# First loads, warm-up and K order at the start of a fused attention and MLP kernel

## The chip, the cores and the metric

The kernel runs on one NeuronCore of a Trainium2 chip. The metric is device time in microseconds (us) for one execution. Three runs of the kernel before gave 262.43, 262.99 and 263.99 us, so its median is 262.99 us.

## What is computed

The input `x` has 2048 rows of 640 numbers in bfloat16. Two branches read it and a gate mixes them:

```
g = sigmoid((x * gate_w).sum(-1))            # one number per row
a = linear_attention(x @ wqkv) @ wo          # 32 heads of 20, phi(q), phi(k)
b = x1 + gelu(layernorm(x1) @ w3) @ w4       # x1 = x + shifted gelu(layernorm(x) @ w1) @ w2
out = g * a + (1 - g) * b
```

with `phi(t) = where(t > 0, t + 1, exp(t)) + 1e-6`. Only the first stage of the attention branch matters here: K = x @ wk, and the gate's sum, which the kernel gets as one more column of the same product.

## The kernel before

**Stages.** The order of all work is written out by hand, with no planner: each engine executes its instructions in the order of the program text, and semaphores join the engines. TensorE (PE) goes through K (line 187), Q (line 233), the attention sums (line 310), then w1, w2, w3, the attention output and w4 in an interleaved order. The rows of `x` are handled in 16 chunks of 128.

**Loads.** Three queues can start transfers: SP (`sp`), ACT (`aq`) and GpSimd, called POOL in the profile (`gq`). A transfer is issued by its engine in program order. At the start the kernel wants natural-layout copies of chunks 0 and 1 of `x` (`load_x`, line 120), the 640-number gate vector as five rows of 128 (`g5`, line 129), and the K weights in five pieces of 128 rows (`load_wk`, line 126). Chunks 2 to 15 come transposed by DMA (`load_xT`, line 123), and behind them SP issues every later weight.

**Turning chunks 0 and 1.** K needs `x` transposed. A DMA transpose of the first chunks would land late, so PE turns chunks 0 and 1 by a product with an identity matrix (`turn`, line 206): five 128-column matmuls a chunk. The results go from PSUM to `xT` in two copies, the first two blocks of a chunk by one engine and the last three by another.

**The gate column.** `g5` is five rows; VectorE (DVE) copies it into a zeroed 128 by 128 tile `g5z` (lines 201 and 202). One small matmul (line 213) turns that into a column of five values in each partition, and ScalarE (ACT) copies it into column 640 of `wk_sb` (line 214). After that `k_mm` (line 183) makes K in two halves of 320 columns, the second with 321, the last of which is the gate's sum for each row. The identity comes from GpSimd (lines 153 and 154).

**Warm-up.** Before any of this PE runs matmuls on constant ones, whose results nobody reads (`warmup`, line 197): five of 512 columns and one of 384.

**Order on PE.** Warm-up; two blocks of chunk 0; the gate matmul; three blocks of chunk 0; five blocks of chunk 1; then K of chunks 0 and 1 by weight piece, pieces 0 to 4 in order, both chunks for each piece; then K of chunks 2 to 15. A PE instruction that waits holds everything behind it.

**Evacuation.** After each chunk `k_evac` (line 190) copies the gate sum out and applies `phi` with one ACT and two DVE instructions.

Of the kernel before, what the change touches and what calls it, by code (L numbers as in the profile page):

```python
# [16 lines left out]
def kernel(  # L17
# [13 lines left out]
    nc = tc.nc  # L31
    P = 128
# [7 lines left out]
    DC = D // P  # L40
# [30 lines left out]
    def pair():  # L71
        return ps.tile([P, 2, 512], F32, name="pp")
# [16 lines left out]
    g5 = const.tile([DC, P], BF16)  # L89
    g5z = const.tile([P, P], BF16)  # L90
# [26 lines left out]
    sp, aq, gq = nc.sync, nc.scalar, nc.gpsimd  # L117

    def load_x(c0, c1, q=sp):
        q.dma_start(x_sb[:, c0:c1, 0:D], x2[c0 * P:c1 * P, :].rearrange("(c p) d -> p c d", p=P))  # L120
# [4 lines left out]
    def load_wk(q, dc):  # L125
        q.dma_start(wk_sb[:, dc, 0:D], A_wqkv[dc * P:(dc + 1) * P, D:2 * D])

    load_x(0, 1)
    aq.dma_start(g5[:], gate_w.rearrange("(c p) -> c p", p=P))
    load_x(1, 2)  # L130
    load_wk(aq, 0)
    load_wk(sp, 1)
    load_wk(aq, 2)
    load_wk(sp, 3)
    load_wk(aq, 4)
    for c0, c1 in ((2, 3), (3, 4), (4, 5), (5, 6), (6, 8), (8, 10), (10, 12), (12, 16)):
        load_xT(c0, c1)
    sp.dma_start(wq_sb, wqkv_v[:, :, 0:D])
# [6 lines left out]
    for g in range(4):  # L145
        if g >= 2:
# [6 lines left out]
    nc.gpsimd.memset(ident[:], 1.0)  # L153
    nc.gpsimd.affine_select(out=ident[:], in_=ident[:], compare_op=ALU.is_equal, fill=0.0,
                            base=0, pattern=[[-1, P]], channel_multiplier=1)
    for c in range(0, NCH, CPT):
        nc.gpsimd.memset(x_sb[:, c:c + CPT, D:D + 1], 1.0)
    nc.gpsimd.memset(hmask[:], 1.0)
# [24 lines left out]
    def k_mm(pt, c, dcs):  # L183
        for dc in dcs:
            for hf in range(2):
                n = HD + hf
                nc.tensor.matmul(pt[:, hf, 0:n], lhsT=xT[:, dc, c * P:(c + 1) * P],  # L187
                                 rhs=wk_sb[:, dc, hf * HD:hf * HD + n], start=(dc == 0), stop=(dc == DC - 1))
# [5 lines left out]
    warm, tp, kps = pair(), pair(), [pair(), pair()]  # L194
    one = nc.const_aps.tensor(1.0, (P, TS), BF16)

    def warmup(n, w=TS):
        for i in range(n):
            nc.tensor.matmul(warm[:, 1, 0:w], lhsT=one[:, 0:P], rhs=one[:, 0:w], start=True, stop=True)

    nc.vector.memset(g5z[:], 0.0)
    nc.vector.tensor_copy(g5z[0:DC, :], g5[:])
    warmup(5)
    warmup(1, 3 * P)

    def turn(pt, c, a, b, copy):
        for dc in range(a, b):
            nc.tensor.matmul(pt[:, 0, (dc - a) * P:(dc - a + 1) * P], lhsT=x_sb[:, c, dc * P:(dc + 1) * P],  # L208
                             rhs=ident[:], start=True, stop=True)
        copy(xT[:, a:b, c * P:(c + 1) * P], pt[:, 0, 0:(b - a) * P].rearrange("p (c s) -> p c s", c=b - a))  # L210
# [2 lines left out]
    nc.tensor.matmul(kps[0][:, 0, 0:DC], lhsT=g5z[:], rhs=ident[:, 0:DC], start=True, stop=True)  # L213
    nc.scalar.copy(wk_sb[:, :, D], kps[0][:, 0, 0:DC])
    turn(kps[1], 0, 2, DC, nc.scalar.copy)
    turn(tp, 1, 0, 2, nc.vector.tensor_copy)
    turn(warm, 1, 2, DC, nc.vector.tensor_copy)
    for dc in range(DC):
        for c in range(2):
            k_mm(kps[c], c, (dc,))  # L220
    for c in range(2):
# [416 lines left out]
```

## Time and profile before

| what | value |
|---|---|
| median of the runs | 262.99 us (262.43 to 263.99) |
| profiled execution, device time | 264.31 us |
| its span, first to last instruction | 262.6 us |
| PE busy | 257.0 us, 98% of the span |
| DVE, ACT, POOL busy | 141.4, 83.3, 26.8 us |
| first matmul | 0.83 us from the span's start |
| first matmul of K | 5.47 us |
| first matmul of Q | 28.75 us |

Times inside the execution are counted from the span's first instruction. Besides the engines' busy times the profile gives a chain: it starts at the last instruction and goes back, step by step, to what released each. "Waits" list how long an engine sat idle and what ended it. A row of a group gives the number of instructions, their summed time and the mean time of one; matmuls overlap, so the distance between starts tells the rate and the listed duration is longer than that distance.

### The profile page before, as it was taken

Reading aid. Unit: us, or ns where it says so; the run is one execution under the profiler, and the core shown is the slowest. Engines: PE = TensorE matmul, PEld = TensorE weight load, DVE = VectorE, ACT = ScalarE, POOL = GpSimd, SP = SyncE. Lnnn points to the kernel's source line nnn. Section 1 sums busy time; section 2 is a strip of 40 time slices with the busy share of each in tenths; the row PEclk is TensorE's granted clock in tenths of the full one; section 3 lists DMA queues with packets and bytes.
Section 4 is the critical chain, followed back from the end, with each engine's and each line's share of the span. In section 5 each row is a group of like instructions: output and inputs, shape, how many; then the busy total and the mean of one; then the engine's idle time right before and its main releaser. Section 6 shows DMA issues by size and latency. Waiting matters only on the chain.

```text
span 262.6 us, 4149 instructions
## 1 busy us (share of the span) xinstructions
PE 257.0 (98%) x1649; PEld 159.4 (61%) x1667; DVE 141.4 (54%) x275; ACT 83.3 (32%) x126; POOL 26.8 (10%) x82
## 2 busy tenths in 40 slices
PE   7999999999999999999999999999999999999995
PEld 3677655688854644555577566567745567555543
DVE  2398778799947895776303478970312223112132
ACT  2455444412164535622420221140233350142100
POOL 3000040012220041031000023310000000000000
PEclk9999999999999999999999999999999999999999
DMA  7999988015656735998002011321200001100011
GB/s 197 182 182 378 365 246 317 0 27 100 125 115 84 189 91 118 180 317 90 6 2 75 25 27 25 75 54 25 76 26 0 0 2 50 50 2 0 0 52 50
DMA packets 47313, 25.78 MB, mean 98 GB/s; under 512 B 35262, under 2 KB 46526, under 8 KB 47294
## 3 DMA queue, kind: packets, MB, share of 16 engines
q1 hardware_dynamic: 46852, 25.03, 38.7%
q10 hardware_dynamic: 442, 0.49, 0.5%
q8 instruction: 13, 0.21, 0.3%
q14 instruction: 6, 0.05, 0.1%
HBM read 13.03 MB, written 3.60 MB: 63 GB/s over the span
## 4 chain that ended last, share of the span: by engine, by line
PE 97%; DMA 1%; issue 0%; SPq 0%; DVE 0%
PE pp L509 22%; PE pp L474 21%; PE pp L187 9%; PE pp L310 8%; PE pp L427 8%; PE pp L458 8%; PE pp L233 8%; PE pp L344 8%; DMA x_sb<-in_A_x_dram 1%; PE pp L518 1%; PE pp L483 1%; PE pp L377 1%; PE pp L363 1%; PE pp L248 0%; PE pp L208 0%
## 5 line engine op out<-in xcount | busy, mean ns | idle before, releaser
L474 PE MATMUL pp<-lnxT,w_sb 128*128 128x512 bf16 x250 | 59.5, 379 | 0.5
L509 PE MATMUL pp<-w_sb,h 128*128 128x384 bf16 (+3 forms) x414 | 57.6, 299 | 0.2 <-issue 0.2
L476 ACT ACTIVATE h<-pp 128x1024 bf16<-128x1024 f32 (+1 forms) x28 | 26.9, 962 | 94.4 <-PE pp L474 94.4
L509 PEld LDWEIGHTS <-h 128*128 128x128 bf16 x416 | 38.3, 98 | 19.4 <-issue 1.2
L474 PEld LDWEIGHTS <-w_sb 128*128 128x128 bf16 x260 | 25.4, 98 | 27.1
L523 DVE SCALAR_TENSOR_TENSOR oc<-pp,omg,x 128x640 bf16<-128x640 f32 (+2 forms) x20 | 14.4, 748 | 45.4 <-PE pp L518 21.2
L461 DVE SCALAR_TENSOR_TENSOR x<-pp,gate,x 128x640 f32<-128x640 f32 x16 | 14.1, 879 | 33.6 <-PE pp L458 33.6
L179 ACT ACTIVATE e<-pp 128x640 bf16<-128x640 f32 (+1 forms) x26 | 21.4, 827 | 9.6 <-PE pp L233 9.6
L458 PE MATMUL pp<-m_sb,pqT 128*128 128x320 bf16 x160 | 24.3, 299 | 0.0
L427 PE MATMUL pp<-w_sb,hsT 128*128 128x320 bf16 x160 | 23.5, 299 | 0.0
L187 PE MATMUL pp<-wk_sb,xT 128*128 128x320 bf16 (+1 forms) x160 | 23.3, 310 | 0.0
L310 PE MATMUL pp<-x_sb,pk 128*128 128x320 bf16 (+1 forms) x160 | 22.0, 300 | 0.0
L233 PE MATMUL pp<-xT,hsT 128*128 128x512 bf16 x98 | 21.6, 379 | 0.1
L310 PEld LDWEIGHTS <-pk 128*128 128x128 bf16 x160 | 18.8, 117 | 3.2
L187 PEld LDWEIGHTS <-xT 128*128 128x128 bf16 x160 | 16.1, 101 | 6.9 <-DVE xT L210 0.2
L427 PEld LDWEIGHTS <-hsT 128*128 128x128 bf16 x160 | 15.6, 98 | 7.7
L458 PEld LDWEIGHTS <-pqT 128*128 128x128 bf16 x160 | 15.7, 98 | 7.7
L280 POOL TENSOR_SCALAR rstd<-mv 128x1 f32<-128x1 f32 (+1 forms) x20 | 7.5, 373 | 116.6 <-DVE mv L286 116.6
L430 DVE TENSOR_TENSOR x<-pp,x_sb 128x640 f32<-128x640 f32 x16 | 13.1, 816 | 10.4 <-PE pp L427 10.3
L344 PE MATMUL pp<-lnxT,w_sb 128*128 128x512 bf16 x77 | 17.9, 379 | 0.2
L233 PEld LDWEIGHTS <-hsT 128*128 128x128 bf16 x100 | 11.8, 118 | 9.7
L180 DVE TENSOR_SCALAR e<-e 128x640 bf16<-128x640 bf16 (+1 forms) x26 | 9.5, 365 | 8.8 <-ACT e L179 7.8
(73 smaller groups left out, 193.8 us busy)
## 6 DMA issues: line engine op xcount, KB each, us to landing
x_sb<-in_A_x_dram SPq DMA_DIRECT2D x1, 2240.0 KB, 11.1
out_dram<-oc SPq DMA_DIRECT2D x14, 160.0 KB, 1.8
w_sb<-in_B_w_dram SPq DMA_DIRECT2D x1, 2160.0 KB, 8.4
w_sb<-in_B_w_dram SPq DMA_DIRECT2D x1, 2080.0 KB
wo_sb<-in_A_wo_dram SPq DMA_DIRECT2D x6, 160.0 KB, 7.2
m_dram<-x SPq DMA_DIRECT2D x3, 320.0 KB, 3.4
hsT<-in_A_wqkv_dram SPq DMA_DIRECT2D x1, 800.0 KB
m_sb<-in_A_wqkv_dram SPq DMA_DIRECT2D x1, 800.0 KB
```

The source lines that it names most:

```text
L179: nc.scalar.activation(ev, src, ACT.Exp)
L187: nc.tensor.matmul(pt[:, hf, 0:n], lhsT=xT[:, dc, c * P:(c + 1) * P], rhs=wk_sb[:, dc, hf * HD:hf * HD + n], start=(dc == 0), stop=(dc == ...
L233: nc.tensor.matmul(pt[:, t % 2, :], lhsT=wq_sb[:, dc, :].rearrange("p (m j) -> p j m", j=DC)[:, j], rhs=xT[:, dc, t * TS:(t + 1) * TS], st ...
L310: nc.tensor.matmul(pt[:, hf, 0:HD + hf], lhsT=w, rhs=x_sb[:, c, hf * HD:(hf + 1) * HD + hf], start=(c == 0), stop=(c == NCH - 1))
L344: nc.tensor.matmul(pt[:, i, :], lhsT=w, rhs=lnxT[t][:, dc, :], start=(dc == 0), stop=(dc == DC - 1))
L427: nc.tensor.matmul(pt[:, hf, 0:HD], lhsT=hsT[:, fc, 2 + c * P:2 + (c + 1) * P], rhs=w2_sb[:, fc, hf * HD:(hf + 1) * HD], start=(fc == 0), ...
L458: nc.tensor.matmul(pt[:, hf, 0:HD], lhsT=pqT[:, j, c * P:(c + 1) * P], rhs=m_sb[:, j, hf * HD:(hf + 1) * HD], start=(j == 0), stop=(j == D ...
L461: nc.vector.scalar_tensor_tensor(x1, pt[:, :, 0:HD], gate[:, c:c + 1], x1, op0=ALU.mult, op1=ALU.add)
L474: nc.tensor.matmul(pt[:, k, :], lhsT=w3_sb[:, dc, fc * P:(fc + 1) * P], rhs=lnT[:, dc, :], start=(dc == 0), stop=(dc == DC - 1))
L476: nc.scalar.activation(h2[:, 2 * i * TS:(2 * i + n) * TS], pt[:].rearrange("p h e -> p (h e)")[:, 0:n * TS], ACT.Gelu_apprx_tanh)
L509: nc.tensor.matmul(dst, lhsT=st[t]["h2"][:, fc * TS + cc * P:fc * TS + (cc + 1) * P], rhs=w4_sb[:, fc, a:b], start=start and fc == 0, stop ...
L523: nc.vector.scalar_tensor_tensor(oc[:, a:b], src, omg[:, c:c + 1], st[t]["x1"][cc][:, a:b], op0=ALU.mult, op1=ALU.add)
```

## The change

The gate vector's load moves from the ACT queue to the GpSimd queue. The K weights' piece 0 becomes the first transfer of the ACT queue, ahead of `x` chunk 1 in the program; pieces 1 and 3 follow on ACT, pieces 2 and 4 go to SP (before: 0, 2, 4 on ACT and 1, 3 on SP). The zeroing and filling of `g5z` move from DVE to GpSimd, where they stand behind the identity and ahead of the remaining small constants. The warm-up becomes six matmuls of 512 columns and one of 256. A further warm-up matmul of 512 columns stands between the turning of chunk 0 and the first K matmuls. K of chunk 0 with piece 0 is now done ahead of the turning of chunk 1; then come chunk 0 with piece 1, chunk 1 with pieces 0 and 1, and both chunks with pieces 3, 2 and 4. The copy of chunk 1's last three blocks moves from DVE to ACT.

```diff
     load_x(0, 1)
-    aq.dma_start(g5[:], gate_w.rearrange("(c p) -> c p", p=P))
+    load_wk(aq, 0)
+    gq.dma_start(g5[:], gate_w.rearrange("(c p) -> c p", p=P))
     load_x(1, 2)
-    load_wk(aq, 0)
-    load_wk(sp, 1)
-    load_wk(aq, 2)
-    load_wk(sp, 3)
-    load_wk(aq, 4)
+    load_wk(aq, 1)
+    load_wk(sp, 2)
+    load_wk(aq, 3)
+    load_wk(sp, 4)
@@
                             base=0, pattern=[[-1, P]], channel_multiplier=1)
+    nc.gpsimd.memset(g5z[:], 0.0)
+    nc.gpsimd.tensor_copy(g5z[0:DC, :], g5[:])
     for c in range(0, NCH, CPT):
         nc.gpsimd.memset(x_sb[:, c:c + CPT, D:D + 1], 1.0)
@@
-    nc.vector.memset(g5z[:], 0.0)
-    nc.vector.tensor_copy(g5z[0:DC, :], g5[:])
-    warmup(5)
-    warmup(1, 3 * P)
+    warmup(6)
+    warmup(1, 2 * P)
@@
     turn(kps[1], 0, 2, DC, nc.scalar.copy)
+    warmup(1)
+    k_mm(kps[0], 0, (0,))
     turn(tp, 1, 0, 2, nc.vector.tensor_copy)
-    turn(warm, 1, 2, DC, nc.vector.tensor_copy)
-    for dc in range(DC):
+    turn(warm, 1, 2, DC, nc.scalar.copy)
+    k_mm(kps[0], 0, (1,))
+    k_mm(kps[1], 1, (0, 1))
+    for dc in (3, 2, 4):
         for c in range(2):
             k_mm(kps[c], c, (dc,))
```

## The prediction

> **What bounds the kernel now.** I read the page's busy line and chain first, then the chain of the first 9 us alone, then the rows of the K line, then the stages of the start one by one.
>
> ```profile
> PE 257.0 (98%) x1649; PEld 159.4 (61%) x1667; DVE 141.4 (54%) x275; ACT 83.3 (32%) x126; POOL 26.8 (10%) x82
> ...
> PE 97%; DMA 1%; issue 0%; SPq 0%; DVE 0%
> ```
>
> PE is the bound over the whole span. The list of PE's waits after 28 us has one entry of 0.2 us, so later stages have nothing to be won or lost by this change but their starting time: what K ends earlier, the kernel ends earlier. The change can only act in the first 10 us.
>
> ```profile
> 7 pieces in order of time: start us, us, what
> 0.73 0.06 issue
> 0.79 0.40 SPq L120
> 1.19 0.06 issue
> 1.25 3.67 DMA x_sb<-in_A_x_dram
> 4.92 0.05 issue
> 4.96 0.71 PE pp L208 x5
> 5.68 3.46 PE pp L187 x16
> ```
>
> The chain there runs through the load of chunk 1 of x, issued at 1.25 and landed at 4.92. Only then does PE turn it, and K begins.
>
> ```profile
> L187 PE MATMUL pp<-wk_sb,xT x160: 297/300/475, 5.5 to 28.5; 128*128 128x320 bf16 x80, 128*128 128x321 bf16 x80
> ```
>
> One line, two durations: the same matmul takes 475 ns early and 300 ns later. The stages show where the step is.
>
> ```profile
> core 0: us, PE busy (x) PEld busy (x) DVE busy (x) ACT busy (x) POOL busy (x), PEclk, DMA share, GB/s
> 0.83:3.80 2.97, 2.97 (x12) 1.32 (x12) 0.45 (x3) 1.07 (x1) 2.14 (x16) 1.00 0.60 157
> 3.80:4.96 1.16, 0.20 (x2) 0.00 (x0) 0.32 (x1) 0.76 (x3) 0.00 (x0) 1.00 1.03 357
> 4.96:5.47 0.51, 0.51 (x5) 0.51 (x6) 0.07 (x1) 0.00 (x0) 0.00 (x0) 1.00 1.04 371
> 5.47:8.15 2.68, 2.68 (x13) 1.46 (x12) 0.81 (x2) 0.00 (x0) 0.00 (x0) 1.00 1.16 218
> 8.15:10.86 2.71, 2.71 (x21) 1.96 (x20) 0.50 (x2) 1.42 (x4) 0.00 (x0) 1.00 0.75 143
> ```
>
> Up to 8.15 us a 320-column matmul starts every 0.267 us (10 starts in 2.68 us; the counts include matmuls that reach over an edge), after it every 0.136 us (20 starts in 2.71 us). So PE ran at half rate until 8.15, although the clock column reads 1.00 throughout; the matmul rows are the ones to trust. PE was busy from 0.83 to 4.00, idle 0.96 us for chunk 1, busy again from 4.96, and was at full rate 3.19 us after that. The first 3.17 us of work, cut by the gap, had not brought full rate.
>
> ```profile
> 0.79 0.56 ACTq L129 DMA_DIRECT2D g<-in_gate_w_dram  x1
> 1.38 1.32 ACTq L126 DMA_DIRECT2D wk_sb<-in_A_wqkv_dram  x3
> ...
> 2.66 0.23 DVE L202 COPY g5z<-g 5x128 bf16<-5x128 bf16 x1 [1.68 <-DMA g<-in_gate_w_dram]
> ```
>
> The gate vector landed at 2.56, 1.77 us after issue, and `g5z` was ready at 2.90; PE wanted it at 3.34.
>
> **The change, part by part.** ACT queue: it loses the gate's issue (0.56 us; piece 0 moves from 1.38 to 0.79). SP still issues two loads of x and two pieces of wk at unchanged times, so its transposes still begin near 2.65. ACT's table load (1.28 us, from 2.73) moves 0.6 earlier and ends near 3.4, off the path of the copies at line 214, which began at 4.03 on its heels. Cost nothing.
>
> The seven 160 KB loads are the same bytes: in 3.80:5.47 the engines move 357 to 371 GB/s, share 1.03, so the last piece cannot land much before its 6.78 now. Their order alters. Piece 0 now runs beside chunk 0 of x. Chunk 0 landed at 3.07; bounds are 3.07 and 4.46 (0.79 plus the 3.67 us of chunk 1, which did share). I take 3.5, nearer the lower, because half of the companion's 160 KB is 0.23 us at 357 GB/s and a little is added for the slowest engine. PE asks for it at 3.56, so it is hidden; beyond that it stalls PE.
>
> GpSimd: DMA issue, a memset (0.20, as `ident`'s row) and a copy are put ahead of the small constants. Those were done at 3.46 and are first read at 50 us (line 310), so their delay costs nothing. The identity stands behind the DMA issue: ready at 1.40 before, wanted at 3.56, it covers 2.1 us. No trace row shows a GpSimd-issued transfer. Bounds for landing are 1.77 us after issue (the ACT one) and 3.9 us (the median of the transposes of x): 2.56 to 4.7. I take 3.5, the middle, since the load now competes with a full DMA stream. The copy on GpSimd takes 0.2 to 0.3 us by the other 128-wide rows there, plus 0.1 as between the landing at 2.56 and DVE's copy at 2.66, so `g5z` is there at 3.85 (2.9 to 5.1). PE asks at 3.77. I take no cost; lateness is the first rival.
>
> The Trainium skill, "DMA: Bandwidth & Descriptors", section "Latency and other measured facts", speaks against this move: first byte after about 1 us for transfers issued from GpSimd and 0.6 us from SP or ACT. An estimate from it is 0.4 us later than the ACT row, 2.96 instead of my 3.5, with `g5z` in time; no run here shows either yet.
>
> PE, at half rate (107 ns for 128 columns, 427 for 512, from the distances of the starts): warm-up 2944 to 3328 columns, +0.32, ends 3.56 instead of 3.24. Two blocks 3.77, gate matmul 3.84, three blocks 4.16, new filler 4.59. K of chunk 0, piece 0: needs the DVE copy (0.42, begun on the second block's end near 4.05, done 4.5) and piece 0, issued 0.59 earlier than its landing at 5.10, so about 4.5: runs 4.59 to 5.12. Chunk 1 turned (landed by 4.92) 5.12 to 5.66. Four pairs for pieces 0 and 1: the first ends 6.19, and chunk 1's need the DVE copy (done near 6.0); ended 7.26. Twelve matmuls more: 10.46, if half rate stayed. In the same way before ends at 5.47 + 20 x 0.267 = 10.83. The 0.96 us idle goes into 0.75 us of unread columns, so the order alone is worth 0.37 us at half rate. With full rate from 8.15 in both, before ends at 9.51 (as in the trace) and after at 8.15 + 2.31 x 0.51 = 9.33: 0.18 us won.
>
> The rest hangs on when full rate comes. The stretch of unbroken work now starts at 0.83 instead of 4.96. Bounds: 0.83 + 3.19 = 4.02, and 8.15 as before. K ends at T + 0.51 x (10.46 - T): 7.30, or 9.33. I take T = 5.7, below the middle (6.1), because the new stretch resembles the one in the trace that worked more than the one that was cut. Then K of two chunks ends at 8.13, 1.38 us before 9.51. Data allows it: the last piece at 6.78 plus four matmuls of 0.136 is 7.3, and the transposed chunk 2 landed at 7.35.
>
> The Trainium skill, "TensorE: Matmul & The Clock Gate", Part 1, says that full rate is granted after a busy window of about 3.4 us, and that these windows run freely, not from the kernel's start. The row agrees as far as it goes: 3.17 us with a gap failed, 3.19 us without succeeded. By that rule an unbroken start at 0.83 opens between 4.2 and 7.7, mean 5.95, an estimate: 1.25 us won instead of 1.38.
>
> Sum: 0.18 for the order and 1.20 for the earlier rate, 1.38 us. The profiled execution took 264.31 (span 262.6, 1.71 outside it) and would take 262.9; the median of the runs stands 1.32 lower than the profiled one, at 262.99, and the same saving gives 261.6. Where the stall for chunk 1 goes: the next late items are piece 4 and the copies of chunk 1.
>
> **Rivals.** *Gate vector late, slower.* PE holds at line 213. If `g5z` comes at G, work restarts there, 6.69 us at half rate remain, and if the stretch is cut, full rate comes at G + 3.19: K ends at G + 4.98. That equals 9.51 at G = 4.53; above it the kernel is slower. At G = 5.85, a landing near 5.5, the loss is 1.3 us; at G = 7 it is 2.5 us and 265.5. For it: no row prices this load, and the traffic of two queues is under way. Against: the ACT row's 1.77 us.
>
> *Chunk 0 late.* At its upper bound, 4.46, PE idles 0.9 us, full rate comes at 7.65 and K ends near 9.5: 263.0, no change.
>
> *The fillers do not count.* Full rate comes at 8.15 again: 262.8. For it: five warm-up matmuls had not earned it before. Against: after the gap barely the same time was enough.
>
> *Everything in time.* T = 4.02: 2.2 us won, 260.8, or somewhat less where the copies of chunk 1 are waited for.
>
> **How the numbers follow.** Half a per cent, 1.3 us, is about what a measurement of this kernel can tell from no change; the three runs alone span 1.56. Chances: forecast 0.42 (its own range 261.0 to 262.2), everything in time 0.13, chunk 0 late 0.12, fillers 0.10, gate late 0.23. Faster by over 0.5%: all of "in time", and three quarters of the forecast, 0.45. Slower by over 0.5%: the gate beyond 5.85, 0.17. The rest, 0.38, within. The range reaches from 260.7 to 264.4, the gate at 5.95.
>
> **What would show it.** Right: no idle between warm-up and K above 0.3 us, the 475 ns rows of K giving way to 300 before 7.7 us, Q beginning near 27.4 instead of 28.75. Wrong: PE idle ahead of line 213 on GpSimd, a GpSimd load that lands after 4.5, half rate lasting to 8 us or beyond.

## The result and the profile after

The changed kernel took 265.35 us (median of 12 runs, 263.79 to 266.02), the kernel before 262.97 us in the same comparison (12 runs, 262.36 to 265.80). The ratio is 1.0074 with a 95% interval of 1.0049 to 1.0098: slower, where faster was forecast, and above the stated range. The profiled execution of the changed kernel is one of its shortest, 263.79 us with a span of 262.1 us. It is still the place to see what the change put on the path.

The chain of the changed kernel over its first 12 us (start, length, what):

```profile
18 pieces in order of time: start us, us, what
...
0.69 0.61 issue
1.30 3.50 DMA g<-in_gate_w_dram
...
4.94 0.28 POOL g5z L157
5.22 0.07 POOL x_sb L159 x2
5.29 0.16 PE pp L213
...
```

Where the load of chunk 1 of x stood, now stands the gate vector: issued by GpSimd at 1.30, landed at 4.80, copied by GpSimd until 5.22. Only then does PE start line 213, the gate matmul. PE's row in the timeline of the same kernel, with the idle time before it in brackets:

```profile
3.83 0.28 PE L208 MATMUL pp<-ident,x_sb 128*128 128x128 bf16 x2
5.27 0.18 PE L213 MATMUL pp<-ident,g5z 128*128 128x5 bf16 x1 [1.16 <-POOL x_sb L159]
```

Two blocks of chunk 0 are turned at 3.83, then PE waits 1.16 us (1.38 between starts). The releaser is printed as a GpSimd memset; the semaphore counts GpSimd's instructions, and the one that matters is the copy of line 157 before it in the chain. And in this execution K ran at full rate from its first matmul:

```profile
L189 PE MATMUL pp<-wk_sb,xT x160: 297/300/310, 5.7 to 27.9; 128*128 128x320 bf16 x80, 128*128 128x321 bf16 x80
```

No K matmul took 475 ns here: starts are 136 ns apart, but for two gaps of about 0.4 us, one where chunk 1 is turned and one right behind it. Full rate had come at 3.79 us, before the wait. That is why this execution is short, and why nine of the twelve, with 265.1 us or more, need an explanation that it does not show.

Two constants tie the start to the result. In all fourteen profiles of this study the device time is 1.7 to 1.8 us above the span, and the span is 253.1 to 253.3 us above the moment when the first two chunks of K are done (the start of the 21st K matmul, called K2 below). So all differences but 0.2 us arise before K2, and a median can be turned into an estimate of its K2: 262.97 is 8.2 us, 265.35 is 10.5 us.

| profile | device us | K begins | full rate from | K2 | Q begins |
|---|---|---|---|---|---|
| before, the one shown at first | 264.31 | 5.47 | 8.15 | 9.52 | 28.59 |
| before, again | 262.55 | 4.45 | 4.03 | 7.75 | 26.82 |
| before, a third time | 265.77 | 4.83 | 3.58 to 7.00, then from 10.41 | 10.91 | 29.99 |
| changed | 263.79 | 5.72 | 3.79 | 8.97 | 28.05 |
| changed, again | 265.39 | 6.07 | 8.81 | 10.42 | 29.49 |

The first row has Q from its first matmul, at 28.59; the 28.75 given for it ahead of the prediction is the start of a piece of the chain, 0.16 us later.

### The profile page after: what moved, and what is told of

Read it like the earlier page. It is cut to its first block, busy times and chain, and to the rows that moved or that the text cites. A ratio compares the mean times of both kernels' runs of the same rounds, so it can differ in the third digit from the quotient of the medians.

```text
span 262.1 us, 4155 instructions
## 1 busy us (share of the span) xinstructions
PE 256.1 (98%) x1651; PEld 158.5 (60%) x1669; DVE 140.5 (54%) x272; ACT 83.9 (32%) x127; POOL 28.2 (11%) x85
## 4 chain that ended last, share of the span: by engine, by line
PE 96%; DMA 1%; issue 1%; DVE 0%; POOL 0%; POOLq 0%
PE pp L513 22%; PE pp L478 21%; PE pp L314 8%; PE pp L431 8%; PE pp L462 8%; PE pp L189 8%; PE pp L237 8%; PE pp L348 8%; DMA g<-in_gate_w_dram 1%; PE pp L522 1%; PE pp L487 1%; PE pp L381 1%; PE pp L367 1%; PE pp L252 0%; DVE xT L210 0%
## 5 line engine op out<-in xcount | busy, mean ns | idle before, releaser
L189 PE MATMUL pp<-wk_sb,xT 128*128 128x320 bf16 (+1 forms) x160 | 22.3, 300 | 0.1
L189 PEld LDWEIGHTS <-xT 128*128 128x128 bf16 x160 | 15.5, 98 | 6.5 <-DVE xT L210 0.4
L183 DVE SCALAR_TENSOR_TENSOR pk<-pp,e 128x640 bf16<-128x640 f32 x16 | 13.2, 825 | 1.7
```

## The experiments

Theory A: the way of the gate vector through GpSimd is the whole loss, by a direct wait and by a cut in the stretch of PE work that earns full rate. Theory B: the other parts (piece 0 of the K weights beside chunk 0 of x, longer warm-up, order of K) cost the time.

### The gate part undone

```diff
+    aq.dma_start(g5[:], gate_w.rearrange("(c p) -> c p", p=P))
     load_wk(aq, 0)
-    gq.dma_start(g5[:], gate_w.rearrange("(c p) -> c p", p=P))
...
-    nc.gpsimd.memset(g5z[:], 0.0)
-    nc.gpsimd.tensor_copy(g5z[0:DC, :], g5[:])
...
+    nc.vector.memset(g5z[:], 0.0)
+    nc.vector.tensor_copy(g5z[0:DC, :], g5[:])
     warmup(6)
```

> The changed kernel with its gate part undone: the gate vector is loaded first on the ACT queue and padded by VectorE as in the kernel before; the order of the K pieces, the longer warm-up, the filler and the order of K stay changed. Theory A (the gate vector's way through GpSimd is the whole loss: PE stood 1.16 us before line 213, restarting at 5.27, and the cut stretch of work brings full rate later in most executions): no wait of PE above 0.3 us before the gate matmul, time 262.2 to 263.0, at or under the kernel before. Theory B (the loss comes from the other parts: chunk 0 sharing the transfer engines with piece 0, the longer warm-up, the split order): time near the changed kernel, 264.8 to 265.8.

Measured: 263.07 us (262.87 to 263.58 in eleven of twelve runs, one of 266.46), the kernel before 263.10; ratio 0.9996 (0.9962 to 1.0031). The loss is gone, 2.28 us under the changed kernel, 0.07 us above what theory A said. With the gate vector back at the head of ACT's queue, piece 0 also goes back behind it, and chunk 0 lands at 3.08 again; what an early piece 0 costs by itself is left to the run with the gate vector second on ACT's queue. The rest of the change (warm-up, filler, order of K) makes no difference that can be told from none: the interval reaches from 1.0 us faster to 0.8 us slower. The stages of this run (PE busy first, the numbers of instructions in brackets):

```profile
core 0: us, PE busy (x) PEld busy (x) DVE busy (x) ACT busy (x) POOL busy (x), PEclk, DMA share, GB/s
0.83:4.62 3.79, 3.79 (x15) 1.62 (x16) 0.72 (x3) 1.73 (x3) 2.11 (x16) 1.00 0.71 207
4.62:5.96 1.34, 1.34 (x10) 0.94 (x9) 0.40 (x1) 0.29 (x2) 0.00 (x0) 1.00 1.12 350
```

PE is busy without a break from 0.83, K begins at 4.62 and full rate comes at 5.96: the course that the prediction had laid out (4.59 and 5.7), and yet no gain.

### The gate part alone

```diff
-    aq.dma_start(g5[:], gate_w.rearrange("(c p) -> c p", p=P))
+    gq.dma_start(g5[:], gate_w.rearrange("(c p) -> c p", p=P))
...
+    nc.gpsimd.memset(g5z[:], 0.0)
+    nc.gpsimd.tensor_copy(g5z[0:DC, :], g5[:])
     for c in range(0, NCH, CPT):
...
-    nc.vector.memset(g5z[:], 0.0)
-    nc.vector.tensor_copy(g5z[0:DC, :], g5[:])
```

> The kernel before with the gate part alone: the gate vector loaded and padded by GpSimd, all else as before. Theory A: PE waits from about 3.4 to about 5.2 us at the gate matmul, chunk 1 is turned behind it, K begins near 6.1 instead of 5.47, and full rate comes later in most executions: 264.3 to 266. Theory B: the gate is hidden behind the wait for chunk 1 (landed at 4.92), 262.8 to 263.4.

Measured: 265.66 us (263.63 to 266.92), ratio 1.0065 (1.0032 to 1.0099). The part alone gives the loss again. It brings piece 0 forward as well, and chunk 0 is turned from 3.91 instead of 3.23. PE by stages in its profile, an execution of 265.86 us:

```profile
core 0: us, PE busy (x), PEclk, DMA share, GB/s
3.45:6.34 2.89, 1.25 (x11) 1.00 1.11 340
6.34:10.34 4.00, 4.00 (x17) 1.00 0.92 152
10.34:13.05 2.71, 2.71 (x21) 1.00 0.95 189
```

From the end of the warm-up at 3.45 to K's start at 6.34 PE worked 1.25 of 2.89 us. Half rate lasted until 10.34 (15 K starts in 4.00 us, then 20 in 2.71). The clock column again reads 1.00 throughout.

### The wait filled with unread work

```diff
+    warmup(3)
     nc.tensor.matmul(kps[0][:, 0, 0:DC], lhsT=g5z[:], rhs=ident[:, 0:DC], start=True, stop=True)
```

> The changed kernel with three more warm-up matmuls of 512 columns (unread results) just ahead of the gate matmul, where PE otherwise waits; the wait for the gate vector stays as it is, only PE works through it. If the cut in the stretch of work, and so the late full rate, is the main cost (theory A, second half): full rate by 7.3 us in every execution, time 262.8 to 263.8, with little spread. If the stall itself is the cost (the work behind the gate matmul begins 1.4 us later, and the rate does not matter): no better than the changed kernel, 265.0 to 265.6.

Measured: 264.06 us, and all twelve runs between 263.96 and 264.33. The gate vector is as late as before (the gate matmul starts at 5.39), only PE no longer idles: full rate comes at 5.98. The first expectation is missed by 0.26 us and the second by 0.94, because both costs are there: of the 2.28 us between the changed kernel and the one with the gate part undone, 1.29 come back when PE keeps working, and 0.99 stay. So by these medians the cut stretch is worth 1.3 us and the direct wait 1.0 us, and the scatter of the changed kernel goes with the cut.

### The gap of the kernel before filled

```diff
+    warmup(2)
     turn(tp, 1, 0, 2, nc.vector.tensor_copy)
```

> The kernel before with two warm-up matmuls of 512 columns (unread results) between the turning of chunk 0 and that of chunk 1, where PE idles 0.96 us for chunk 1; nothing else is changed. If an unbroken stretch of work brings full rate earlier: the slow executions of the kernel before (263.99 and 264.31 among its runs) go, median 262.2 to 262.7. If the gap did not matter in most executions: 262.8 to 263.2, with the same scatter.

Measured: 263.12 us (262.32 to 264.05) beside 263.10 (262.35 to 265.77); ratio 0.9985 (0.9958 to 1.0013). The median does not move. Above 264.2 us there are none of its 12 runs and 9 of the 35 of the kernel before. Filling the gap seems to take away long executions, but it does not improve the median. Why not, this run does not show: its filler ends at 4.65, while chunk 1 landed at 4.49 here and at 3.98 and 4.20 in two later profiles of the kernel before, so the filler itself can hold PE back by what an early full rate wins.

### Only the load undone

```diff
+    aq.dma_start(g5[:], gate_w.rearrange("(c p) -> c p", p=P))
     load_wk(aq, 0)
-    gq.dma_start(g5[:], gate_w.rearrange("(c p) -> c p", p=P))
```

> The changed kernel with the load of the gate vector alone undone: ACT loads it first, GpSimd still pads it. If the load by GpSimd is the part that is late (theory A, narrowed): the vector lands near 2.1, the copy on GpSimd (0.28 us) is done by 2.9, the gate matmul finds it ready, 262.8 to 263.3 as with the whole gate part undone (263.07). If the padding on GpSimd costs by itself: PE waits at the gate matmul and the time is 264 or more.

Measured: 263.26 us (263.01 to 264.10 in eleven of twelve, one of 266.16), ratio 1.0002 (0.9973 to 1.0032). GpSimd's padding is harmless; the timeline of GpSimd shows it done at 2.56, over a microsecond before PE asks:

```profile
2.28 0.28 POOL L157 COPY g5z<-g 5x128 bf16<-5x128 bf16 x1 [0.72 <-DMA g<-in_gate_w_dram]
```

Of the gate part, then, the move of the load makes the loss and the padding does not.

### The gate matmul later in PE's order

The kernel with the gate part alone, and then:

```diff
     turn(tp, 0, 0, 2, nc.vector.tensor_copy)
-    nc.tensor.matmul(kps[0][:, 0, 0:DC], lhsT=g5z[:], rhs=ident[:, 0:DC], start=True, stop=True)
-    nc.scalar.copy(wk_sb[:, :, D], kps[0][:, 0, 0:DC])
     turn(kps[1], 0, 2, DC, nc.scalar.copy)
     turn(tp, 1, 0, 2, nc.vector.tensor_copy)
+    nc.tensor.matmul(kps[0][:, 0, 0:DC], lhsT=g5z[:], rhs=ident[:, 0:DC], start=True, stop=True)
+    nc.scalar.copy(wk_sb[:, :, D], kps[0][:, 0, 0:DC])
```

> The kernel before with the gate vector loaded and padded by GpSimd, as in the run of the gate part alone (265.66), but with the gate matmul moved two matmuls behind the arrival of chunk 1 in PE's order, so that only three small matmuls and K stand behind it. Theory A: the wait is then mostly hidden by that for chunk 1, K begins near 5.9 instead of 6.34, 263.1 to 264.0. If a transfer issued by GpSimd costs time in another way than through the wait at this matmul: 265 or more, as with the gate part alone.

Measured: 265.01 us (263.40 to 265.69), ratio 1.0047 (1.0018 to 1.0075): a miss, the number is the rival's. The waits of PE in its profile (264.59 us):

```profile
PE pp L208 <- DMA x_sb<-in_A_x_dram: 0.3, 1, 0.3
PE pp L215 <- POOL x_sb L159: 0.3, 1, 0.3
PE pp L208 <- DVE xT L210: 0.2, 1, 0.2
```

The long wait has become three short ones, one of them for chunk 0, which now shares the transfer engines with piece 0. K began at 5.80, as expected. Full rate came at 8.14, and K2 is 9.66, against 9.52 in the first profile of the kernel before, whose full rate came at 8.15. At equal full rate the kernel is thus 0.14 us later, in line with theory A. That most of its executions have late full rate is suggested by nine of twelve times of 264.59 or more, but only this one was profiled; a further cost of the GpSimd transfer is not excluded.

### No warm-up

```diff
-    warmup(5)
-    warmup(1, 3 * P)
```

> The kernel before without any warm-up matmul. No work on the path to K moves: PE turns chunk 0 when it lands, and K begins near 5.5 as before. Only the stretch of work that earns full rate begins some 2.4 us later and is cut at once by the wait for chunk 1. If full rate is earned by an uncut stretch: it comes between 8 and 12 us in every execution, the two first chunks of K end 1 to 2 us later than in the common execution of before, 264.3 to 266. If the rate comes at a time of its own: 262.8 to 263.3.

Measured: 264.25 us (263.64 to 266.82), ratio 1.0047 (1.0014 to 1.0079), at the lower edge of what was expected. The profiled one is the second shortest, 263.65 us: PE's first matmul at 3.17, K from 4.76, full rate at 7.49, earlier than the 8 to 12 that were expected. Nothing on the path to K moved to later, so the unread work earns about 1.1 us (0.4 to 2.1 by the interval), most likely by bringing full rate earlier.

### The same load in a quiet moment

```diff
         if t == 0:
             pt = pair()
             w3_rest((0, 1), (pt[:, 0, 0:LT], pt[:, 1, 0:LT]))
+        if t == 1:
+            gq.dma_start(g5b[:], gate_w.rearrange("(c p) -> c p", p=P))
+            nc.gpsimd.tensor_copy(g5z[0:DC, :], g5b[:])
         w4_tile(t)
```

> The changed kernel with the same load of the gate vector issued once more by GpSimd near 170 us, when the transfer engines are nearly idle, into a tile of its own; GpSimd waits for it and copies it, nothing else does. If the 3.5 us from issue to landing at the start are contention with the seven 160 KB loads: the second lands in under 2.2 us. If they are the price of a transfer issued by GpSimd as such: 3 us or more again. The time is that of the changed kernel, 263.8 to 266.

The time is 263.93 us, one execution. The row of this second load (line, count, duration, KB, median us to landing) is from the list of transfers of that kernel, the row after it from that of the changed kernel at its start:

```profile
g5b<-in_gate_w_dram POOLq DMA_DIRECT2D x1, 1.2 KB, 2.1
```

```profile
g<-in_gate_w_dram POOLq DMA_DIRECT2D x1, 1.2 KB, 3.5
```

Issued by GpSimd, the 1.2 KB land after 2.1 us in quiet and after 3.5 us beside the seven 160 KB loads: 1.4 us goes with the company at the start, whether by contention or by a first use. The ACT row of the kernel before was 1.77 us, issued ahead of the company. One load was timed in each place.

### The kernel before, profiled again

> The kernel before, unchanged, profiled once more. The forecast was made on an execution of 264.31 us in which full rate came at 8.15 us, and took that for the usual one. If the usual execution of the kernel before (262.4 to 263.4) has full rate early in spite of its gap: full rate between 4 and 6.5 us, span 260.9 to 261.7, first matmul of Q near 27.3. If full rate always comes about 8 us there, and the execution of 264.31 was long for another reason: first matmul of Q at 28.6 again.

> The same kernel and the same question once more, since about one execution in five of the kernel before is a long one.

The first execution took 262.55 us, 0.4 to 0.7 us under the medians of the kernel before, with full rate at 4.03, span 260.8 and Q at 26.82, half a microsecond earlier than expected. The K line there, and the turning of chunk 1:

```profile
L187 PE MATMUL pp<-wk_sb,xT x160: 297/300/309, 4.4 to 26.7; 128*128 128x320 bf16 x80, 128*128 128x321 bf16 x80
```

```profile
4.17 0.44 PE L208 MATMUL pp<-ident,x_sb 128*128 128x128 bf16 x5 [0.17 <-DVE xT L210]
```

No 475 ns at all, and not "in spite of its gap": PE sat idle for 0.17 us ahead of chunk 1 and not for 0.96, since chunk 1 landed at 3.98. In the seven profiles with the gate vector first on ACT's queue it landed at 3.98 to 4.92, and the 4.92 of the profile on which the forecast stands is the latest. That profile was not the usual course of the kernel, in its loads as in its rate. The second execution took 265.77 us, for a reason that no theory had: piece 1 of the K weights landed at 7.11, PE waited 1.61 us for it, and the rate went back to half. PE by stages, clock column after the busy time:

```profile
core 0: us, PE busy (x), PEclk, DMA share, GB/s
3.58:7.00 3.42, 1.45 (x14) 1.00 1.37 250
7.00:10.41 3.41, 3.25 (x13) 0.50 0.80 167
10.41:13.05 2.64, 2.64 (x21) 1.00 1.04 161
```

### The gate vector second on ACT's queue

```diff
     load_wk(aq, 0)
-    gq.dma_start(g5[:], gate_w.rearrange("(c p) -> c p", p=P))
+    aq.dma_start(g5[:], gate_w.rearrange("(c p) -> c p", p=P))
```

with the padding back on VectorE.

> The changed kernel with the gate vector loaded by ACT right behind K's piece 0, ahead of pieces 1 and 3, and padded by VectorE: piece 0 stays the first transfer of the ACT queue. Theory A: the vector is issued near 1.2, lands in 2.1 to 2.8 us by the GpSimd rows and the ACT ones, so 3.0 to 3.9, is padded by 3.3 to 4.3, and PE wants it at 3.8: a wait of 0 to 0.5 us, and 263.0 to 263.8, nearer the kernel before than the changed one. If the order of the loads (piece 0 ahead of the gate vector) costs by itself: 264.5 or more.

Measured: 263.62 us (263.37 to 264.16), ratio 1.0016 (0.9994 to 1.0038). VectorE starts the copy at 3.99, the gate matmul starts at 4.23, K at 4.98, full rate comes at 5.72. As expected: the same 1.2 KB, issued behind piece 0 by ACT, are copied 0.95 us earlier than by way of GpSimd (3.99 instead of 4.94), and the kernel is 1.7 us faster than the changed one. It is 0.36 us behind the kernel before (by the interval 0.2 us ahead to 1.0 behind), so an early piece 0 does not make the loss by itself, although chunk 0 was turned only from 3.97. From issue to copy the vector took 2.78 us here (1.21 to 3.99), against 1.87 at the head of ACT's queue (0.79 to 2.66): the company costs a load by ACT too.

### The changed kernel, profiled again

> The changed kernel, unchanged, profiled once more. Its one profile so far is of a short execution (263.79 us), in which full rate came at 3.79 us, ahead of the wait at the gate matmul; nine of its twelve executions took 265.1 us or more. If these are the ones in which the wait falls into the stretch that must earn full rate: an execution of 265 to 266 us, half rate until 7 to 10.5 us, first matmul of Q near 29.3 to 30. If it is again a short one, full rate before 4.7 us. If a long one shows full rate early: the theory of the cut stretch is wrong for this kernel.

This execution took 265.39 us, a usual execution of the changed kernel (one of the kernel before, taken beside it, was a long one of 265.41). PE's stages between the turning of chunk 0 and K2:

```profile
core 0: us, PE busy (x) PEld busy (x) DVE busy (x) ACT busy (x) POOL busy (x), PEclk, DMA share, GB/s
3.79:5.32 1.53, 0.40 (x3) 0.14 (x3) 0.43 (x1) 0.00 (x0) 0.34 (x5) 1.00 1.01 346
5.32:6.07 0.75, 0.75 (x6) 0.47 (x7) 0.00 (x0) 0.36 (x2) 0.61 (x8) 1.00 3.02 230
6.07:8.81 2.74, 2.74 (x15) 1.76 (x14) 0.42 (x1) 0.77 (x2) 0.94 (x6) 1.00 0.76 152
8.81:11.50 2.69, 2.69 (x21) 1.93 (x20) 0.33 (x1) 1.16 (x4) 0.00 (x0) 1.00 0.83 165
```

The same wait as in the short execution, 3.79 to 5.32, but here full rate had not come before it. It comes at 8.81, 3.49 us after work restarts. K2 is 10.42 against 8.97 in the short one: 1.45 us between two executions of one kernel, from the rate alone but for 0.05 us in the gate matmul's start.

No version that was tried is measurably faster than the kernel before.

## Why the prediction was wrong

Two steps failed. "I take no cost" for the gate vector is the one that made the kernel slower; "the same saving gives 261.6" is why no gain is left even when that cost is taken away (263.07 against 263.10 us).

**The gate vector was 1.3 to 1.4 us later than forecast, outside the bounds.** The step "I take 3.5, the middle" had the landing between 2.56 and 4.7; it was 4.80, 4.84 and 4.94 in the three profiles of the changed start, and PE waited 1.16, 1.13 and 1.03 us where "I take no cost" stood. Two terms were too small. GpSimd starts the issue at 1.30, where ACT and SP start theirs at 0.79, so 0.51 us went before it began; the bounds had no room for that. Then came 3.5 us where 2.7 had been taken, inside the bounds of 1.77 and 3.9; 2.1 of them are the quiet price and 1.4 the start's company. The copy was priced nearly right (0.28 plus 0.14 us). The Trainium skill's "DMA: Bandwidth & Descriptors", section "Latency and other measured facts", had pointed the right way with its 1 us against 0.6 for the first byte, but the estimate from it, 2.96 us for the landing, was further off than the one from rows.

**The first rival came true, and its formula held where the stretch was cut.** "K ends at G + 4.98": the profile of 265.39 us has the gate matmul at 5.32, so 10.30; K2 measured 10.42. The mechanism and the place were right. It had been given a chance of 0.23, and the loss that it reckoned was too small, as the next point shows.

**The base was the wrong execution.** "The same saving gives 261.6" carried a saving from a profile with full rate at 8.15 to a median 1.32 us lower. Those 1.32 us are as large as the saving that was forecast: by its time the median execution has K2 at 8.2, and the forecast K2 for the changed kernel was 8.13. No execution at the median was profiled; the one of 262.55 us shows full rate at 4.03 and chunk 1 at 3.98 in place of 8.15 and 4.92. The unbroken stretch came out as laid out in the run with the gate part undone (full rate 5.96, K2 8.26), and gained nothing against a usual course that was already there. With the usual K2 of 8.2 in place of 9.51 the first rival turns slower from G = 3.2 and not from 4.53, and at G = 5.32 it costs 2.1 us and not 0.8; 2.4 us were measured.

**The idle time that was to go was not what it looked like.** The 0.96 us for chunk 1 belongs to the execution that was profiled first; in the two later ones PE waited 0.17 and 0.38 us there. The place was filled in two runs without a change of the median. That a long wait there makes a part of the long executions of the kernel before, by late full rate as in the first profile, fits the run with the gap filled but is not shown.

**What held.** The small constants on GpSimd cost nothing, the identity was ready at 2.68 and wanted at 3.8, and ACT's table load ended at 3.46 (forecast 3.4). Chunk 0 beside piece 0 was not quite hidden: it came at 3.78, 0.2 us after the warm-up's end (forecast 3.5). "Fillers do not count" is refuted by the filled wait and by the kernel without warm-up.

**What stays open.** Why full rate comes early in one execution and late in the next is not shown by a run of its own. In the kernel before the idle time differed; in the changed kernel the wait at the gate matmul was the same in both profiles (1.16 and 1.13 us), and full rate came ahead of it in one and behind it in the other. The clock records and the stages fit an account by fixed stretches of 3.41 us that begin at another moment in each execution: 3.58 to 7.00 to 10.41 in one profile. In twelve others the record of full rate lasts 256.00 or 259.41 us, 75 or 76 times 3.413. How much work a stretch needs is open, for the busy times do not settle it: by this account 2.75 of 3.41 us were enough in the third profile of the kernel before (0.17 to 3.58), and 2.87 were not in the run with the gate matmul later (1.32 to 4.73). The Trainium skill's "TensorE: Matmul & The Clock Gate", Part 1, gives 3413 ns for such a window, free-running. By it the wait at the gate matmul costs the rate unless a window ends before most of the wait has passed; full rate came at 3.79 and 4.63 us in the two profiles of the changed start that were short, the first of the changed kernel and the one with the second load (263.93 us).

## What to carry to other kernels

A transfer that stands at the head of PE's order should be priced from the same issuing engine under the same company, and if no row shows that, the forecast belongs near the late bound. Before a saving is carried from one profiled execution to the median, see whether the profile is a usual one: here it lay 1.3 us above it, and that difference was as large as the forecast gain. An early wait on PE can cost twice: here 1.0 us by itself and 1.3 us by the late full rate that follows.

## What had not been expected

Full rate can be lost again by idle times of under 2 us. In the third profile of the kernel before, PE was busy 1.45 of the 3.42 us from 3.58 to 7.00, and the next 3.41 us ran at half rate. In the short execution of the changed kernel PE was busy 2.13 of the 3.41 us from 3.79 to 7.20, and full rate stayed. The Trainium skill's "TensorE: Matmul & The Clock Gate", section "Why this matters for your kernels", allows gaps up to about 3 us and names one idle window as what brings half rate back; here 1.97 us of idle time within 3.42, most of it one wait of 1.61 us, were enough.

The clock column of a stage reads 1.00 while PE still runs at half rate before its first record, in all profiles here, and 0.50 only when full rate had been granted once. The distance between matmul starts, 267 against 136 ns for 320 columns, is the measure to go by.
